# A list-scheduled opening for a T5 attention and bilinear feed-forward kernel, with pair 7 inside it and pads on two engines

## The chip, the cores and the metric

One core of a Trainium2 chip. The metric is device time in microseconds (us) of that core. The kernel before takes 417.34 us (median of 3 runs, 416.81 to 418.78).

## The reference

```python
# q, k, v: [8 batches, 8 heads, 576, 64]; bias_table: [32, 8]
scores = q @ k.T / 8 + bias_table[bucket(|i - j|)]       # T5 relative bias
attn   = softmax(scores) @ v
x      = attn.transpose(0, 2, 1, 3).reshape(4608, 512)   # [tokens, heads * 64]
out    = ((x @ w_a) * (x @ w_b)) @ w_out                 # d_ff = 1536
```

The kernel works on pairs of heads: pairs 0 to 3 are batch 0, 4 to 7 batch 1, up to 31. The softmax bias is a multiplication by exp(bias) after the exponential.

Of the kernel before, what the change touches and what calls it, by code (L numbers as in the profile page):

```python
# [13 lines left out]
def kernel(  # L14
# [11 lines left out]
    nc = tc.nc  # L26
# [7 lines left out]
    NM = 4  # L34
# [60 lines left out]
    vm = [wpool.tile([128, H, NM, Dh + 1], BF16, name=f"vm{i}") for i in range(2)]  # L95
    vt = [wpool.tile([128, H // 2, 2, Dh + 1], BF16, name=f"vt{i}") for i in range(2)]

# [70 lines left out]
    def load_vt(b):  # L168
        for hh in range(2):
            nc.gpsimd.dma_start(  # L170
                out=vt[b % 2][64 * hh:64 * hh + 64, :, hh, 0:Dh],
                in_=v[b, hh:H:2, SM:S, :].transpose([1, 0, 2]))
# [31 lines left out]

# [7 lines left out]
    nc.vector.memset(zero_sb[:, :], 0.0)  # L212
# [26 lines left out]

    nc.sync.dma_start(out=tab.ap(), in_=tab_sb[0:H, :])  # L240
    pad_vt(0)
    pad_ones(0)

# [5 lines left out]
    def load_vt_part(b, hh):  # L249
        nc.gpsimd.dma_start(  # L250
            out=vt[b % 2][64 * hh:64 * hh + 64, :, hh, 0:Dh],
            in_=v[b, hh:H:2, SM:S, :].transpose([1, 0, 2]))
# [85 lines left out]
    def copy_k(p, eng):  # L338
        copy(eng, KT[p % 4][:, :, :], st[p]["tk"][:, 0:SM].rearrange("d (t c) -> d t c", t=NM))

    def t_q(p, eng=None):
        if p >= NP or not early(p // 4):
            return
        ps = tr_half()
        transposes(ps, qn, p)
        copy(eng, QT[p % 4][:, :, :].rearrange("d a c -> d (a c)").rearrange("d (p t) -> d p t", t=NM),
             ps[:, 0:SM].rearrange("d (t p) -> d p t", t=NM))

    def t_k(p, eng=None, pool=None):
        if p >= NP or not early(p // 4):  # L350
            return
        ps = pool.tile([128, 1024], BF16, tag="ffn", name=f"trk{p}") if pool else tr_half()
        transposes(ps, kn, p)
        copy(eng, KT[p % 4][:, :, :], ps[:, 0:SM].rearrange("d (t c) -> d t c", t=NM))

# [198 lines left out]
    def av_mm(p, jqs, pool=None, tag="av"):  # L554
        b, hp = divmod(p, 4)
        i = b % 2
        pav = (pool or ps_av).tile([128, 3, 2, Dh + 1], FP32, tag=tag, name=f"av{p}_{jqs[0]}")
        for slot, jq in enumerate(jqs):
            nc.tensor.matmul(out=pav[:, slot, :, :], lhsT=weights_tail(p, jq),  # L559
                             rhs=vt[i][:, hp, :, :], start=True, stop=True)  # L560
            if jq == 4:
                for t in range(NM):
                    nc.tensor.matmul(out=pav[:, slot, :, :], lhsT=weights_last(p, t),  # L563
                                     rhs=vm[i][:, 2 * hp:2 * hp + 2, t, :], start=False,
                                     stop=True, skip_group_check=True)
# [25 lines left out]
    def t_x(p, jqs=range(5), eng=None):  # L591
        b, hp = divmod(p, 4)
        c0 = SM * B + ST * b
        if 4 <= p < NP - 1 and p != 7:
            nc.sync.dma_start_transpose(
# [77 lines left out]
    def ff_o_out(c, tt):  # L673
        ob = wrk.tile([128, DM], FP32, tag="ob", name=f"ob{c}_{tt}")
        nc.scalar.activation(out=ob[:, :], in_=ff["po", tt][:, :], func=ACTF.Copy)  # L675
# [15 lines left out]
    for c in range(NCH):  # L691
        if c == 0:
            parts = [(range(0, 8), 0, 256), (range(0, 8), 256, 256), (range(8, NDF), 0, 512)]
        else:
            parts = [(range(NDF), 0, 512)]
# [22 lines left out]
    def v_next(s):  # L718
# [9 lines left out]
    opening = """  # L728
        <k0 <q0 <q123h0 <tk <k23 <k1 <W0 <v0 <vtb <Wtb <W1 <W3 <vta <W2 <tq <R1 <q123h1 <v1 <R0 <Wta
        <wa0 <wb0 TK0 PD0 CK0:A PD1 w1 TQ0 PU1 CQ00:D CQ01:D w4 S000 w2 PU0 TQ20 E000 PC1 TQ10 S001 CQ20:D  # L730
        CQ10:D TQ30 E001 PC0 TZ1 CQ30:D S011 CZ1:A PC2 <vt1b <uq <vt1a <R2 <wa1 <q4 <R3 <k4 <wb1 <vb1b
        <q5 <k5 <uk <vb1a <wb2 <q6 <q7 <k6 <k7 <wa2 <wo S010 PF0 TK3 PF1 E011 TK2 CK3:D CK2:D E010 w1
        S300 M001 TK1 E300 M000 KS CK1:D EK w1 S101 V0:D E101 w1 S100 E100 M101 w1 S200 AV00 M300 E200 S301
        N00 TZ0 E301 M100 X00 S201 CX00:D AV10 wa4 E201 M200 N10 CZ0:A M201 X10 TQ11 M301 CX10:A T0 CQ11:A
        V1:D TQ31 ET0 S111 M010 AV20 E111 PW MT0 T1 N20 AV30 CQ31:A ET1 M011 TQ21 LH S110 N30 X20 CQ21:A
        S310 CX20:A MT1 X30 E110 AV01 CX30:D M111 FA0a E310 M110 S210 FB0a N01 HA0a S211 E210 FA1a G0a
        AV11 HA1a M210 E211 X01 T2 N11 TZ0x CX01:A T3 ET2 FB1a M211 X11 FA2a G1a CX11:A S311 MT2 HA2a
        FB2a ET3 CZ0x:D AV21 G2a E311 M310 TQ4 FA3a N21 CQ4:A TK4 FB3a HA3a CK4:D X21 FA4a G3a CX21:A
        S41 M311 HA4a S43 E41 MT3 FB4a FA5a E43 G4a AV31 LV M41 HA5a S40 V3:D S42 N31 E40 FB5a TQ5 G5a
        E42 X31 FA6a CQ5:D FB6a HA6a CX31:D TK5 G6a TZ1x CK5:A FA7a M40 FB7a HA7a CZ1x:D S52 S53 G7a E52  # L740
        FA0b V2:D FB0b M42 HA0b T4 E53 G0b FA1b M52 FB1b HA1b S50 M53 ET4 FA2b G1b TQ6 M43 HA2b S51
        CQ6:A FB2b MT4 E51 TQ7 G2b AV40 CQ7:D E50 TK6 M51 TK7 CK6:A FA3b M50 FB3b HA3b CK7:D S61 G3b T5
        E61 N40 FA4b FB4b HA4b M61 T6 ET5 G4b AV41 FA5b ET6 N41 TH S63 FB5b MT5 HA5b S62 E63 FA6b G5b MT6
        AV50 HA6b M63 E62 S60 FB6b N50 E60 FA7b G6b AV51 M62 HA7b FB7b M60 FA8f G7b N51 FB8f HA8f G8f
    """
# [4 lines left out]
    def step(token):  # L750
# [185 lines left out]
```

## The kernel before, where the change touches it

The first two batches are written out by hand as a list of tokens, executed in program order: each engine works through its own share of the list in that order. A tile scheduler puts in the waits. After the list comes a loop over the pairs `s`, which interleaves attention with nine feed-forward units for each pair.

```python
    vt = [wpool.tile([128, H // 2, 2, Dh + 1], BF16, name=f"vt{i}") for i in range(2)]
    ...
    def pad_vt(i):                                   # zeros beside V's tails, on DVE
        nc.vector.memset(vt[i][0:64, :, 1, :], 0.0)
        nc.vector.memset(vt[i][64:128, :, 0, :], 0.0)
    ...
    trb = ps_tr.tile([128, 1024], BF16, tag="tr", name="trb")   # one PSUM tile, used in halves
    def tr_half():
        turn[0] ^= 1
        return trb[:, 512 * turn[0]:512 * turn[0] + 512]
    ...
    def t_x(p, jqs=range(5), eng=None):
        ...
        if 4 <= p < NP - 1 and p != 7:               # pairs 4, 5, 6, 8 .. : by DMA transpose
            nc.sync.dma_start_transpose(out=xn_sb[hp][...], in_=XG[p % 2][...])
            ...
            return
        tr_x(p, jqs)                                 # the others: by PE and a copy
        copy_x(p, jqs, eng)
    ...
    opening = """
        <k0 <q0 <q123h0 <tk <k23 <k1 <W0 <v0 <vtb <Wtb <W1 <W3 <vta <W2 <tq <R1 <q123h1 <v1 <R0 <Wta
        <wa0 <wb0 TK0 PD0 CK0:A PD1 w1 TQ0 PU1 CQ00:D CQ01:D w4 S000 w2 PU0 TQ20 E000 PC1 TQ10 S001 CQ20:D
        CQ10:D TQ30 E001 PC0 TZ1 CQ30:D S011 CZ1:A PC2 ... S010 PF0 TK3 PF1 E011 TK2 CK3:D CK2:D E010 w1
        ... AV10 wa4 E201 M200 N10 ... FA0a E310 M110 S210 FB0a N01 HA0a ...
        ... AV51 M62 HA7b FB7b M60 FA8f G7b N51 FB8f HA8f G8f
    """
    ...
    for s in range(7, NP + 1):                       # pairs 7 .. 31, then the rest
        ...
```

How to read a token. `<x` starts a load. `TQ`, `TK`, `TZ`, `X` are transposes on PE (of queries, keys, tails, results), `CQ`, `CK`, `CZ`, `CX` their copies out of PSUM, with `:A` on ACT and `:D` on DVE. `S` are scores (PE), `E` their exponential (ACT), `M` the multiplication by the bias (DVE). `KS`, `EK` and `T`, `ET`, `MT` do the same for the 64 tail rows and columns. `AV` is the product with V, `N` its division by the sums (DVE). `FA`, `FB` are the feed-forward products pa and pb, `HA` (ACT) and `G` (DVE) join them; `w` are fill matmuls on zeros; `P…` write constant pads. `TH` starts batch 2's DMA transposes (among them QB, its queries), and the loop's first pair of batch 2 is pair 8.

The softmax here doesn't subtract the row's maximum and nothing guards it: scores larger than these inputs give would overflow.

## Time and profile before

| profile of the kernel before | us |
|---|---|
| first score (S000) | 6.97 |
| first pa / first pb of the feed-forward | 26.18 / 27.94 |
| first score of pair 8 | 73.69 |
| pair 8 to the end | 340.52 |
| span | 414.2 |

These milestones, from PE's timeline, cut the run into a start, a hand-written second half, and a loop both kernels share. The page's head says how full PE is (busy us, share, instructions):

```profile
span 414.2 us, 8826 instructions
...
PE 403.8 (97%) x3497; PEld 210.9 (51%) x3497; DVE 241.1 (58%) x568; ACT 251.3 (61%) x388; POOL 133.5 (32%) x191
```

PE has nearly no free time, so a change must cut PE's work, or the waits in the first 28 us. This is how ACT opens, in order of time (start, length, engine, line, operation; in brackets the idle time before and what ended it):

```profile
7.41 1.02 ACT L452 ACTIVATE ath<-qkh 128x1024 bf16<-128x1024 f32 x1 [1.40 <-PE qkh L446]
8.64 1.02 ACT L452 ACTIVATE ath<-qkh 128x1024 bf16<-128x1024 f32 x1 [0.21 <-PE qkh L446]
10.15 0.77 ACT L296 ACTIVATE ZB<-trb 64x256 bf16<-64x256 bf16 x2 [0.49 <-DVE QT L298]
10.94 2.86 ACT L452 ACTIVATE ath<-qkh 128x1024 bf16<-128x1024 f32 x3
```

The exponentials are `ath<-qkh`, 1.02 us each.

### The profile page before, as it was taken

The numbers are of one execution on the slowest core, as the hardware profiler recorded it, in microseconds if no ns is written. First come the engines' busy times: TensorE is split into PE (matmuls) and PEld (weight loads), VectorE is DVE, ScalarE is ACT, GpSimd is POOL, SyncE is SP. The second block draws the span as 40 slices with busy tenths as digits, with TensorE's granted clock in tenths as the row PEclk, the third lists the DMA queues.
The fourth block names the chain that finished last, engine by engine and source line by source line (L and its number), as shares of the span: only waits on it lengthen the run. The fifth ranks groups of instructions, "written<-read, shape, count | busy, mean of one in ns | idle before, by whom it ended". The sixth has DMA issues, their size and how long they took to land.

```text
span 414.2 us, 8826 instructions
## 1 busy us (share of the span) xinstructions
PE 403.8 (97%) x3497; PEld 210.9 (51%) x3497; DVE 241.1 (58%) x568; ACT 251.3 (61%) x388; POOL 133.5 (32%) x191
## 2 busy tenths in 40 slices
PE   8789999999999999999999999999999999999996
PEld 3467664545454455544555555554545555444443
DVE  5778887466764665477646774567646652421320
ACT  4988876486647676676667665866476742322321
POOL 7956546399209500870059003400000000000000
PEclk9999999999999999999999999999999999999999
DMA  9999999999949943996099707940421012002004
GB/s 116 171 210 191 205 157 144 164 142 138 123 96 163 121 82 71 150 128 112 15 162 157 112 16 140 124 92 17 101 82 16 17 40 78 0 2 102 1 2 101
DMA packets 135786, 42.05 MB, mean 102 GB/s; under 512 B 113688, under 2 KB 130968, under 8 KB 135744
## 3 DMA queue, kind: packets, MB, share of 16 engines
q0 software_dynamic: 81712, 20.27, 54.6%
q1 hardware_dynamic: 48592, 11.87, 18.1%
q10 hardware_dynamic: 5440, 9.34, 6.8%
q8 instruction: 27, 0.44, 0.5%
q14 instruction: 15, 0.12, 0.1%
HBM read 39.18 MB, written 9.45 MB: 117 GB/s over the span
## 4 chain that ended last, share of the span: by engine, by line
PE 90%; DMA 3%; POOL 2%; ACT 2%; issue 1%; ACTq 0%; DVE 0%
PE pb L633 23%; PE pa L633 23%; PE po L670 22%; PE av L569 7%; PE qk L406 7%; DMA wb<-in_moe_w_b_dram 3%; PE av L559 2%; PE av L563 2%; PE qkt L479 1%; POOL W L235 1%; DMA bias_tab<-wo 1%; PE trb L306 1%; PE trb L415 1%; PE warm L220 1%; ACT att L514 1%
## 5 line engine op out<-in xcount | busy, mean ns | idle before, releaser
L430 ACT ACTIVATE at<-qk 128x1024 bf16<-128x1024 f32 x112 | 113.5, 1030 | 26.4 <-PE qk L406 10.6
L643 DVE TENSOR_TENSOR g<-pb,ha 128x512 bf16<-128x512 f32 (+1 forms) x116 | 75.9, 654 | 74.7 <-PE pb L633 46.8
L633 PE MATMUL pb<-xn,wb 128*128 128x512 bf16 (+1 forms) x464 | 112.5, 365 | 0.8 <-DMA wb<-in_moe_w_b_dram 0.8
L633 PE MATMUL pa<-xn,wa 128*128 128x512 bf16 (+1 forms) x464 | 112.5, 365 | 0.0
L640 ACT ACTIVATE ha<-pa 128x512 f32<-128x512 f32 (+1 forms) x116 | 66.7, 575 | 65.0 <-PE pa L633 65.0
L670 PE MATMUL po<-wo,g 128*128 128x512 bf16 x420 | 99.0, 379 | 0.0
L435 DVE TENSOR_TENSOR at<-at,W 128x1024 bf16<-128x1024 bf16 x112 | 74.8, 684 | 18.2 <-ACT at L430 18.2
L633 PEld LDWEIGHTS <-wa 128*128 128x128 bf16 x464 | 42.0, 98 | 46.2 <-issue 6.0
L633 PEld LDWEIGHTS <-wb 128*128 128x128 bf16 x464 | 41.4, 97 | 43.0 <-issue 4.7
L670 PEld LDWEIGHTS <-g 128*128 128x128 bf16 x420 | 38.7, 98 | 44.0 <-issue 2.5
L675 ACT ACTIVATE ob<-po 128x512 f32<-128x512 f32 x35 | 21.1, 601 | 40.7 <-PE po L670 34.4
L569 PE MATMUL av<-vm,at 128*128 128x65 bf16 x896 | 41.2, 194 | 0.0
L170 POOL DMA_DIRECT2D vt<-in_v_dram x12 | 7.4, 621 | 104.1 <-PE av L563 103.2
L580 DVE RECIPROCAL rc<-av 128x6 f32<-128x6 f32 (+1 forms) x64 | 11.9, 186 | 49.5 <-PE av L569 43.8
L569 PEld LDWEIGHTS <-at 128*128 128x128 bf16 x896 | 37.2, 98 | 6.2
L132 POOL DMA_DIRECT2D qn<-in_q_dram x48 | 36.8, 832 | 9.9 <-PE pb L633 6.8
L141 POOL DMA_DIRECT2D kn<-in_k_dram x48 | 36.4, 820 | 2.0 <-PE pb L633 1.4
L559 PE MATMUL av<-vt,att 128*128 128x130 bf16 x152 | 33.3, 219 | 0.0
L406 PE MATMUL qk<-QB,KB 64*128 64x512 bf16 x192 | 29.2, 381 | 0.2 <-ACT att L506 0.2
L582 DVE TENSOR_TENSOR XG<-av,rc 128x384 bf16<-128x384 f32 (+1 forms) x64 | 27.1, 424 | 2.2
L506 ACT ACTIVATE att<-qkt 128x640 bf16<-128x640 f32 x24 | 16.9, 702 | 12.9 <-PE qkt L480 12.9
L559 PEld LDWEIGHTS <-att 128*128 128x128 bf16 x152 | 15.0, 98 | 6.4
(104 smaller groups left out, 325.2 us busy)
## 6 DMA issues: line engine op xcount, KB each, us to landing
out_dram<-ob ACTq DMA_DIRECT2D x32, 256.0 KB, 2.6
vn<-in_v_dram POOLq DMA_DIRECT2D x16, 256.0 KB, 5.6
kn<-in_k_dram POOLq DMA_DIRECT2D x48, 64.0 KB, 4.6
qn<-in_q_dram POOLq DMA_DIRECT2D x48, 64.0 KB, 4.3
wa<-in_moe_w_a_dram POOLq DMA_DIRECT2D x3, 512.0 KB, 9.3
wb<-in_moe_w_b_dram POOLq DMA_DIRECT2D x3, 512.0 KB, 10.4
wo<-in_moe_w_out_dram POOLq DMA_DIRECT2D x1, 1536.0 KB, 15.5
xn<-XG SPq DMA_TRANSPOSE x52, 4.1
```

Source lines behind the costliest of these rows:

```text
L132: nc.gpsimd.dma_start(out=by_tile(qn[b % 2])[:, h0 // 4, t, :, :], in_=q[b, h0:h1, 128 * t:128 * t + 128, :].transpose([1, 0, 2]))
L141: nc.gpsimd.dma_start(out=by_tile(kn[b % 2])[:, h0 // 4, t, :, :], in_=k[b, h0:h1, t:SM:NM, :].transpose([1, 0, 2]))
L406: nc.tensor.matmul(out=ps[:, hh, :], lhsT=kT[r, t, :], rhs=qT[r, :, :], start=True, stop=True)
L430: nc.scalar.activation(out=at[:, :, :], in_=ps[:, :, :], func=ACTF.Exp, scale=scale)
L435: nc.vector.tensor_tensor(out=at[:, :, :], in0=at[:, :, :], in1=w[:, :, S - 1 + t:S - 1 + t - SM:-1], op=MULT)
L559: nc.tensor.matmul(out=pav[:, slot, :, :], lhsT=weights_tail(p, jq), rhs=vt[i][:, hp, :, :], start=True, stop=True)
L569: nc.tensor.matmul(out=pav[:, slot, hh, :], lhsT=weights(p, t, hh, jq), rhs=vm[i][:, 2 * hp + hh, t, :], start=False, stop=True, skip_grou ...
L582: nc.vector.tensor_tensor(out=xg[:, jqs[0]:jqs[0] + m, :, :], in0=pav[:, 0:m, :, 0:Dh], in1=rc[:, 0:m, :].unsqueeze(3).to_broadcast([128, ...
L633: nc.tensor.matmul(out=ps[:, 0:n], lhsT=w[df // 4][:, mc, 128 * (df % 4):128 * (df % 4) + 128], rhs=xn_sb[mc][:, 512 * c + lo:512 * c + lo ...
L640: nc.scalar.activation(out=ha[:, 0:n], in_=ff["pa", df, lo][:, 0:n], func=ACTF.Copy)
L643: nc.vector.tensor_tensor(out=g_sb[df][:, lo:lo + n], in0=ff["pb", df, lo][:, 0:n], in1=ff["ha", df, lo][:, 0:n], op=MULT)
L670: nc.tensor.matmul(out=po[:, :], lhsT=g_sb[df][:, 128 * tt:128 * tt + 128], rhs=wo_sb[:, df, :], start=(df == 0), stop=(df == NDF - 1))
```

## The change

It replaces the hand order of the opening by that of a list scheduler: exponentials close together at the start, 22 fills cut to 13, fewer changes of tile form, pair 7 wholly inside the opening, another load order, and pads that either copy engine can write. The diff, cut to its core (helpers, dead code and most tokens left out):

```diff
-    vt = [wpool.tile([128, H // 2, 2, Dh + 1], BF16, name=f"vt{i}") for i in range(2)]
+    vt = [wpool.tile([128, 2, H // 2, Dh + 1], BF16, name=f"vt{i}") for i in range(2)]
 ...
+    def pad(eng, x, p0, p1):
+        if eng is nc.vector:
+            nc.vector.memset(x, 0.0)
+            return
+        ...
+        nc.scalar.activation(out=x, in_=z, func=ACTF.Copy)      # z: a view of the zeros
 ...
-        if 4 <= p < NP - 1 and p != 7:
+        if 4 <= p < NP - 1:
 ...
-            parts = [(range(0, 8), 0, 256), (range(0, 8), 256, 256), (range(8, NDF), 0, 512)]
+            parts = [(range(0, 6), 0, 256), (range(0, 6), 256, 256), (range(6, NDF), 0, 512)]
 ...
     opening = """
-        <k0 <q0 <q123h0 <tk <k23 <k1 <W0 <v0 <vtb <Wtb <W1 <W3 <vta <W2 <tq <R1 <q123h1 <v1 <R0 <Wta
-        <wa0 <wb0 TK0 PD0 CK0:A PD1 w1 TQ0 PU1 CQ00:D CQ01:D w4 S000 w2 PU0 TQ20 E000 PC1 TQ10 S001 CQ20:D
+        <k0 <q0 <tk <q123h0 <k23 <k1 <tq <vta <R0 <W1 <vtb <W0 <q123h1 <v0 <W3 <W2 <v1 <Wta <Wtb <k4 <R1
+        <uq <wa0 <wb0 ... PV0:A PF1:D PF0:D TK0 PV1:D TQ0 CQ00:D PU1:A w1 TZ1 CK0:A CQ01:A PX1:D S000 E000 PC1:D
+        CZ1:D S001 E001 TQ30 S011 TQ10 TK3 PX0:D CK3:D TK2 E011 CQ10:D CK2:D PU0:D S010 CQ30:A S301 TK1
 ...
+        S210 E210 S211 E211 M110 TQ31 LH N01 MT1 X01 T2 ET2 N30 AV11 CQ31:D X30
+        CX30:A T3 ET3 CX01:D S311 FA0a HA0a N11 E311 TZ0x FB0a ...
 ...
+        E73 M73 AV51 N51 TH T7 M72 ... AV70 ... N70 AV60 ... X70 ... AV71 CX70:D ... CX71:A ... FO02 HO0
 ...
-    for s in range(7, NP + 1):
+    for s in range(8, NP + 1):
```

More of the change, by code (lines that the diff above doesn't have):

```diff
@@ L170, in load_vt @@
             nc.gpsimd.dma_start(
-                out=vt[b % 2][64 * hh:64 * hh + 64, :, hh, 0:Dh],
+                out=vt[b % 2][64 * hh:64 * hh + 64, hh, :, 0:Dh],
                 in_=v[b, hh:H:2, SM:S, :].transpose([1, 0, 2]))
@@ L191, in pad_tl, with pad_vt, pad_blocks, pad_x @@
         nc.vector.memset(tl[i][64:128, :, :, 0:Dh], 0.0)
-    def pad_vt(i):
-        nc.vector.memset(vt[i][0:64, :, 1, :], 0.0)
-        nc.vector.memset(vt[i][64:128, :, 0, :], 0.0)
+    def pad(eng, x, p0, p1):
+        if eng is nc.vector:
+            nc.vector.memset(x, 0.0)
+            return
+        n = int(np.prod(x.shape[1:]))
+        z = (zero_sb.bitcast(FP32) if x.dtype == FP32 else zero_sb)[p0:p1, 0:n]
+        if len(x.shape) == 3:
+            z = z.rearrange("p (a b) -> p a b", b=x.shape[2])
+        elif len(x.shape) == 4:
+            z = z.rearrange("p (a b c) -> p a b c", b=x.shape[2], c=x.shape[3])
+        nc.scalar.activation(out=x, in_=z, func=ACTF.Copy)
+    def pad_vt(i, hh, eng):
+        pad(eng, vt[i][64 * hh:64 * hh + 64, 1 - hh, :, :], 64 * hh, 64 * hh + 64)
+    def pad_blocks(x, hh, eng):
+        o = (Dh - Dh * hh) // 2
+        pad(eng, x.bitcast(FP32)[64 * hh:64 * hh + 64, :, :, o:o + Dh // 2], 64 * hh, 64 * hh + 64)
     def pad_ones(i):
-        nc.vector.memset(vt[i][0:64, :, 0, Dh:Dh + 1], 1.0)
-        nc.vector.memset(vt[i][64:128, :, 1, Dh:Dh + 1], 1.0)
+        nc.vector.memset(vt[i][0:64, 0, :, Dh:Dh + 1], 1.0)
+        nc.vector.memset(vt[i][64:128, 1, :, Dh:Dh + 1], 1.0)
         nc.vector.memset(vm[i][:, :, :, Dh:Dh + 1], 1.0)
-    def pad_x(i):
-        nc.vector.memset(XG[i][64:128, 4, :, :], 0.0)
+    def pad_x(i, eng):
+        pad(eng, XG[i][64:128, 4, :, :], 64, 128)
     nc.sync.dma_start(out=bt_sb[0:NB, :], in_=bias_table)
@@ L213 @@
     nc.vector.memset(tab_sb.bitcast(FP32)[0:H, :], TWO_ONES)
+    pad_ones(0)
+    pad_ones(1)
     nc.vector.tensor_tensor(out=bt_sb[0:NB, :], in0=bt_sb[0:NB, :], in1=bl_sb[0:NB, :],
@@ L240 @@
     nc.sync.dma_start(out=tab.ap(), in_=tab_sb[0:H, :])
-    pad_vt(0)
-    pad_ones(0)
     def load_wt(hh):
@@ L250, in load_vt_part @@
         nc.gpsimd.dma_start(
-            out=vt[b % 2][64 * hh:64 * hh + 64, :, hh, 0:Dh],
+            out=vt[b % 2][64 * hh:64 * hh + 64, hh, :, 0:Dh],
             in_=v[b, hh:H:2, SM:S, :].transpose([1, 0, 2]))
@@ L339, in copy_k @@
         copy(eng, KT[p % 4][:, :, :], st[p]["tk"][:, 0:SM].rearrange("d (t c) -> d t c", t=NM))
-    def t_q(p, eng=None):
-        if p >= NP or not early(p // 4):
-            return
-        ps = tr_half()
-        transposes(ps, qn, p)
-        copy(eng, QT[p % 4][:, :, :].rearrange("d a c -> d (a c)").rearrange("d (p t) -> d p t", t=NM),
-             ps[:, 0:SM].rearrange("d (t p) -> d p t", t=NM))
-    def t_k(p, eng=None, pool=None):
-        if p >= NP or not early(p // 4):
-            return
-        ps = pool.tile([128, 1024], BF16, tag="ffn", name=f"trk{p}") if pool else tr_half()
-        transposes(ps, kn, p)
-        copy(eng, KT[p % 4][:, :, :], ps[:, 0:SM].rearrange("d (t c) -> d t c", t=NM))
     tz = {}
@@ L559, in av_mm @@
             nc.tensor.matmul(out=pav[:, slot, :, :], lhsT=weights_tail(p, jq),
-                             rhs=vt[i][:, hp, :, :], start=True, stop=True)
+                             rhs=vt[i][:, :, hp, :], start=True, stop=True)
             if jq == 4:
@@ L673, in ff_o_out @@
     def ff_o_out(c, tt):
-        ob = wrk.tile([128, DM], FP32, tag="ob", name=f"ob{c}_{tt}")
+        ob = ob_last if (c, tt) == (0, 2) else wrk.tile([128, DM], FP32, tag="ob", name=f"ob{c}_{tt}")
         nc.scalar.activation(out=ob[:, :], in_=ff["po", tt][:, :], func=ACTF.Copy)
@@ L728 @@
     opening = """
-        <k0 <q0 <q123h0 <tk <k23 <k1 <W0 <v0 <vtb <Wtb <W1 <W3 <vta <W2 <tq <R1 <q123h1 <v1 <R0 <Wta
-        <wa0 <wb0 TK0 PD0 CK0:A PD1 w1 TQ0 PU1 CQ00:D CQ01:D w4 S000 w2 PU0 TQ20 E000 PC1 TQ10 S001 CQ20:D
-        CQ10:D TQ30 E001 PC0 TZ1 CQ30:D S011 CZ1:A PC2 <vt1b <uq <vt1a <R2 <wa1 <q4 <R3 <k4 <wb1 <vb1b
-        <q5 <k5 <uk <vb1a <wb2 <q6 <q7 <k6 <k7 <wa2 <wo S010 PF0 TK3 PF1 E011 TK2 CK3:D CK2:D E010 w1
-        S300 M001 TK1 E300 M000 KS CK1:D EK w1 S101 V0:D E101 w1 S100 E100 M101 w1 S200 AV00 M300 E200 S301
@@ L734 @@
-        N00 TZ0 E301 M100 X00 S201 CX00:D AV10 wa4 E201 M200 N10 CZ0:A M201 X10 TQ11 M301 CX10:A T0 CQ11:A
-        V1:D TQ31 ET0 S111 M010 AV20 E111 PW MT0 T1 N20 AV30 CQ31:A ET1 M011 TQ21 LH S110 N30 X20 CQ21:A
-        S310 CX20:A MT1 X30 E110 AV01 CX30:D M111 FA0a E310 M110 S210 FB0a N01 HA0a S211 E210 FA1a G0a
-        AV11 HA1a M210 E211 X01 T2 N11 TZ0x CX01:A T3 ET2 FB1a M211 X11 FA2a G1a CX11:A S311 MT2 HA2a
-        FB2a ET3 CZ0x:D AV21 G2a E311 M310 TQ4 FA3a N21 CQ4:A TK4 FB3a HA3a CK4:D X21 FA4a G3a CX21:A
@@ L739 @@
-        S41 M311 HA4a S43 E41 MT3 FB4a FA5a E43 G4a AV31 LV M41 HA5a S40 V3:D S42 N31 E40 FB5a TQ5 G5a
-        E42 X31 FA6a CQ5:D FB6a HA6a CX31:D TK5 G6a TZ1x CK5:A FA7a M40 FB7a HA7a CZ1x:D S52 S53 G7a E52
-        FA0b V2:D FB0b M42 HA0b T4 E53 G0b FA1b M52 FB1b HA1b S50 M53 ET4 FA2b G1b TQ6 M43 HA2b S51
-        CQ6:A FB2b MT4 E51 TQ7 G2b AV40 CQ7:D E50 TK6 M51 TK7 CK6:A FA3b M50 FB3b HA3b CK7:D S61 G3b T5
-        E61 N40 FA4b FB4b HA4b M61 T6 ET5 G4b AV41 FA5b ET6 N41 TH S63 FB5b MT5 HA5b S62 E63 FA6b G5b MT6
@@ L744 @@
-        AV50 HA6b M63 E62 S60 FB6b N50 E60 FA7b G6b AV51 M62 HA7b FB7b M60 FA8f G7b N51 FB8f HA8f G8f
+        <k0 <q0 <tk <q123h0 <k23 <k1 <tq <vta <R0 <W1 <vtb <W0 <q123h1 <v0 <W3 <W2 <v1 <Wta <Wtb <k4 <R1
+        <uq <wa0 <wb0 <q4 <R3 <q7 <R2 <k5 <q5 <k6 <wa1 <vt1b <uk <wb1 <k7 <vt1a <q6 <vb1a <wa2 <wb2
+        <vb1b <wo PV0:A PF1:D PF0:D TK0 PV1:D TQ0 CQ00:D PU1:A w1 TZ1 CK0:A CQ01:A PX1:D S000 E000 PC1:D
+        CZ1:D S001 E001 TQ30 S011 TQ10 TK3 PX0:D CK3:D TK2 E011 CQ10:D CK2:D PU0:D S010 CQ30:A S301 TK1
@@ new lines @@
+        E010 E301 CK1:D TQ20 CQ20:D M011 M010 w1 S100 E100 M100 TZ0 CZ0:D S101 E101 M101 w2 S300 E300 w2
+        S200 KS TQ11 M001 TQ21 M000 E200 V0:D CQ11:D S201 EK M300 T0 M301 E201 ET0 AV00 N00 CQ21:A M201
+        S110 AV10 S111 N10 X00 X10 E110 M200 T1 V1:A AV20 CX00:A PW:D MT0 CX10:A TK4 N20 E111 AV30 CK4:A
+        AV01 ET1 M111 X20 CX20:A S210 E210 S211 E211 M110 TQ31 LH N01 MT1 X01 T2 ET2 N30 AV11 CQ31:D X30
+        CX30:A T3 ET3 CX01:D S311 FA0a HA0a N11 E311 TZ0x FB0a FA1a CZ0x:D G0a X11 TQ4 HA1a S310 CX11:A
@@ new lines @@
+        MT3 CQ4:D M311 FB1a G1a E310 M310 FA2a M211 HA2a TQ7 CQ7:A S43 M210 E43 S41 E41 FB2a G2a FA3a
+        TK5 TQ5 AV31 CQ5:D FB3a S42 N31 CK5:A S51 HA3a MT2 M43 FA4a X31 TK6 E42 HA4a E51 G3a CK6:D AV21
+        LV CX31:A S52 E52 N21 S53 E53 PC0:D FB4a G4a FA5a TK7 X21 HA5a FB5a M42 S50 E50 CX21:D S40 FA0b
+        G5a FB0b HA0b CK7:D M41 TQ6 E40 G0b TZ1x CZ1x:D FA1b HA1b S71 CQ6:D FB1b E71 G1b V2:D FA2b HA2b
+        T4 ET4 M40 FB2b G2b S70 MT4 FA3b FB3b M51 T6 HA3b AV40 E70 FA4b HA4b M71 T5 G3b N40 M53 FB4b G4b
@@ L745 @@
+        FA5b ET5 MT5 HA5b AV41 ET6 FB5b G5b FA6f FB6f N41 HA6f S61 E61 S72 FA7f E72 HA7f M52 M50 AV50
+        G6f M70 M61 V3:A FB7f N50 S73 S62 FA8f MT6 G7f E73 M73 AV51 N51 TH T7 M72 FB8f HA8f G8f E62 M62
+        S63 ET7 MT7 FA9f S60 E63 FB9f HA9f M63 E60 AV70 G9f M60 FA10f FB10f HA10f N70 AV60 G10f N60 X70
+        FA11f HA11f AV71 CX70:D FB11f FO00 N71 AV61 X71 CX71:A G11f N61 FO01 FO02 HO0
     """
@@ L819, in step @@
             av_norm(p, jqs)
-            if not first and i[1] == 1:
+            if 4 <= p < 7 and i[1] == 1:
                 t_x(p)
@@ L825, in step @@
             copy_x(p, jqs, eng)
+        elif kind == "PV":
+            pad_vt(0, p, eng)
+        elif kind == "PC":
+            pad_vt(1, p, eng)
         elif kind == "PU":
-            pad_z(1, p)
+            pad_blocks(ZB[1], p, eng)
         elif kind == "PF":
-            nc.vector.memset(tl[0][64 * p:64 * p + 64, :, :, Dh - Dh * p:128 - Dh * p], 0.0)
-        elif kind == "PC":
-            if p == 2:
-                pad_ones(1)
-            else:
-                nc.vector.memset(vt[1][64 * p:64 * p + 64, :, 1 - p, :], 0.0)
+            pad_blocks(tl[0], p, eng)
+        elif kind == "PX":
+            pad_x(p, eng)
         elif kind == "PW":
-            nc.vector.tensor_copy(out=Wt_sb[:, :, 0:64], in_=Wt_sb[:, :, 64:128])
-        elif kind == "PD":
-            pad_x(p)
+            copy(eng, Wt_sb[:, :, 0:64], Wt_sb[:, :, 64:128])
         elif kind == "LH":
@@ L851 @@
     pad_tl(1)
-    quotas = {7: 9, 8: 9}
     load_slot = {bb: 9 if bb == 3 else 12 if bb == 4 else 4 * bb - 5 for bb in range(3, B)}
-    for s in range(7, NP + 1):
+    for s in range(8, NP + 1):
         new = s < NP
         U = "unit"
-        A = lambda *jq: (lambda: av(s - 1, jq))
+        A = lambda *jq: (lambda: av(s - 1, jq) if s > 8 else None)
         steps = []
@@ L862 @@
         if new:
-            head = [U, lambda: ex(s, 1), A(0, 1, 2), U, lambda: mul(s, 0), lambda: t_q(s + 1), U,
+            head = [U, lambda: ex(s, 1), A(0, 1, 2), U, lambda: mul(s, 0), U,
                     lambda: mul(s, 1)]
@@ L866 @@
             if s == 8:
-                late = [A(3, 4), U, lambda: t_x(7, (0, 1, 2)), U, lambda: t_x(7, (3, 4))]
-            if shared(s):
-                pair = [lambda: v_next(s), lambda: (qk(s, 2), ex(s, 2), ex_rows(s)), U,
-                        lambda: ex(s, 3), U, lambda: mul(s, 2), lambda: mul_rows(s)]
-            else:
-                pair = [lambda: v_next(s), lambda: (qk(s, 2), ex(s, 2)), U, lambda: ex(s, 3),
-                        lambda: t_k(s + 1, ACT), U, lambda: mul(s, 2)]
+                late = [U]
+            pair = [lambda: v_next(s), lambda: (qk(s, 2), ex(s, 2), ex_rows(s)), U,
+                    lambda: ex(s, 3), U, lambda: mul(s, 2), lambda: mul_rows(s)]
             tail = [lambda: (qk_tail(s), ex_tail(s)), U, U, lambda: mul_tail(s)]
@@ L893 @@
                     load_half(bb, g)
-        quota = quotas.get(s, 9)
+        quota = 9
         seen, put = 0, 0
```

## The prediction

> **What bounds the kernel now.** I read the page's chain of work first, then stretches of each engine, then the tensor engine in order of time, then the load queue. The chain is matmuls almost throughout:
>
> ```profile
> PE 90%; DMA 3%; POOL 2%; ACT 2%; issue 1%; ACTq 0%; DVE 0%
> ```
>
> The stretches (columns: length, then busy us of PE, PEld, DVE, ACT, POOL; clock; DMA share; GB/s) tell where it is not:
>
> ```profile
> 7.00:16.00 9.00, 6.78 (x95) 3.68 (x94) 5.51 (x18) 7.86 (x10) 8.93 (x13) 1.00 1.19 170
> 16.00:26.00 10.00, 8.80 (x166) 6.51 (x165) 9.19 (x25) 8.99 (x16) 7.17 (x11) 1.00 1.21 183
> 28.00:40.00 12.00, 11.81 (x166) 8.72 (x166) 9.72 (x27) 9.11 (x19) 8.95 (x13) 1.00 1.35 198
> 64.00:74.00 10.00, 10.00 (x88) 5.11 (x86) 6.76 (x16) 5.92 (x10) 4.88 (x7) 1.00 1.70 153
> ```
>
> From 7 to 26 us no engine is full alone: ACT has 7.86 of 9, then DVE 9.19 of 10, and PE's busy time contains fill matmuls on zeros. From 28 us PE is full. So only the first 28 us hold much to win. Three places of PE's timeline cut the run (start, length, engine, line):
>
> ```profile
> 1.19 2.31 PE L220 MATMUL warm<-zero_sb 128*128 128x512 bf16 x5 [1.19 <-DVE zero_sb L212]
> ...
> 26.18 0.60 PE L633 MATMUL pa<-xn,wa 128*128 128x256 bf16 x4
> 26.71 0.39 PE L446 MATMUL qkh<-QT,KT 64*128 64x256 bf16 x4
> 27.94 0.61 PE L633 MATMUL pb<-xn,wb 128*128 128x256 bf16 x4 [0.83 <-DMA wb<-in_moe_w_b_dram]
> ...
> 73.69 0.61 PE L406 MATMUL qk<-QB,KB 64*128 64x512 bf16 x4
> ```
>
> They are PE's first matmul; the first pb of the feed-forward, which waits for wb; and the first score of pair 8, from which both programs run the same loop. Busy time hides gaps, since ends are modelled. So I took the spacing with which each kind of matmul follows itself in the trace (512 columns 216 ns, 256: 109, 130: 57, 128: 55.5, 65: 32, 64: 29; two half-array matmuls side by side count once) and added 96 ns for each change of tile form (a 256-column matmul before a 64-row one takes 205 ns instead of 109). By this count PE's own work is 19.08 us up to the first pb and 43.69 us from there to pair 8. The trace took 26.75 and 45.75. So 7.67 us of waiting lie before the first pb and 2.06 us after it; after pair 8 I count 1.3 us in 326 us.
>
> [...] The first five fills follow one another at 427 ns, the same fill from 6 us at 216[...]. [...] the trace's 64x256 ACT copies took 0.38. [...] the stretches show 170 to 214 GB/s from 5 to 55 us, and wb, issued at 17.43 us, landed only at 27.89.
>
> **The change, part by part.** From the compiled order of both programs:
> - Fills. 22 fill matmuls before pair 8 become 13: 9 x 0.216 = 1.94 us less PE work.
> - Grouping. Changes of tile form before pair 8 fall from 81 to 68: 13 x 0.096 = 1.25 us less.
> - Pair 7's products with V and its transposes move ahead of pair 8: 1.82 us of PE work that leave the loop. Nothing is saved by the move itself.
> - The split of chunk 0 (6 instead of 8 blocks by halves) keeps the columns.
> So PE's work to the first pb is 19.10 (as good as 19.08, fewer fills but more attention), from there to pair 8 42.26 (43.69 before), and over the program 3.2 us less. If waits stayed as they are the gain would be 3.2 us.
>
> - Pads. One 64x260 and one 64x256 memset (0.28 and 0.27 us on DVE) go to ACT, before its first exp, while ACT is idle (1.40 and 2.22 us idle in the trace): free. The ones move into DVE's wait of 0.91 us for the bias row, also free.
> - Scores. ACT's first three exps start at 7.41, 8.64 and 10.94 us now; fills, a transpose and the key-tail copies stand between. Afterwards S000, S001, S011 are adjacent and the tail copies are DVE's: I expect about 7.3, 8.2, 9.1. ACT's twelfth item of this sort then comes about 1.1 us earlier. But batch 0's third-pair keys (k23, landing 9.69) hold TK3 and what stands behind it.
> - Loads. W0 was 7th in the queue, v0 8th; now they are 12th and 14th. I map landing time to bytes queued ahead, from the trace: 896 KB 10.37 us, 1282 KB 12.90, 1540 KB 15.07, 1832 KB 16.01, 2248 KB 18.58, 2760 KB 21.46, 3272 KB 24.36, 3784 KB 27.89, 4072 KB 29.06. The new order puts W0 at 1444 KB, about 14.0 us (was 10.73), v0 at 1892 KB, 16.3 us (was 12.90), and, as k4 and the batch 1 query tails (192 KB) now stand before the first weights, wb at 3976 KB, 28.7 us (was 27.89).
> - DVE's chain. Its first bias multiplications need W0: they ran at 11.83 us, now not before 14.0. It then has, in order up to N30 (the last quarter of batch 0's first half): 12 multiplications at 0.605 = 7.3, the norms 3.2, two tail multiplications 1.4, copies, tails and values 2.5, together 14.2 to 14.5 us, so N30 ends near 28.3, its transpose and ACT copy near 28.9. The first pa starts near 29 (26.18 before), the first pb near 29.3 (27.94 before): 1.36 us later, although ACT is ahead.
>
> After that DVE has about 39 us of work in PE's 44 (it is at 10.77 of 12 in its fullest stretch now); the loads for pairs 5 to 7 and the later weights land, by the same map, at or just before their use (wa1 36.3, wb1 39.6, k7 40.3 us against needs at about 36.4, 39.7 and 40.5). I leave the waits there at 2.0 us.
>
> The sum: first pb +1.36; work to pair 8 42.26 - 43.69 = -1.43; waits there -0.06; pair 7's work off the loop -1.82. Together -1.95 us: 417.34 - 1.95 = 415.4 us.
>
> **Rivals.** (a) The start is bound by ACT and the rearranged exps carry through: DVE's 14 us were read too pessimistically or W0 lands near 12.5, and pb waits for wb only. Then pb starts near 28.0 to 28.7 and, with 1 us of waits after it, the span falls by 3.5 to 4.2 us: about 413.3. For it: ACT is at 7.86 of 9 and 8.99 of 10. Against it: DVE at 9.19 of 10 with the loads earlier than they will be. (b) New waits in the second half: pair 7 inside the opening must write XG while pair 5's DMA transposes (5 to 8 us from issue to landing in the trace) still read it, and batch 2's transposes are issued after pair 5's, some 10 us before pair 8; each could cost 1 to 2 us, for about 418. For it: the transpose of the queries took 7.7 us from issue. Against it: the author put two feed-forward blocks before N70. (c) Fewer fills let the clock fall back while DVE waits for W0[...], 417 to 418. For it: PE's work between the first score and the first product with V is 7.0 us in a stretch of about 12. [...]
>
> **Range and chances.** The gain cannot pass 2% (8.3 us): all waiting before pair 8 is 9.7 us, and wb's landing near 28 keeps about 8 us of it unless the load queue itself gets faster. A loss of 2% would need three rivals at once. Predicted 415.4 us; 412.6 to 417.9 should hold it 8 times in 10. Chances: faster by over 2% 0.03, within 2% 0.95, slower 0.02.
>
> **What would show it.** In the changed profile: fills down by nine; first exps at 7.3, 8.2, 9.1; DVE idle before its first bias multiplication near 14 us, named as waiting for W; first pa near 29 and first pb near 29.3, DVE full between; PE from there to pair 8 in about 44.3 us; the loop from pair 8 1.8 us shorter. If pb starts before 28 us, or pair 8 later than 75 us, the steps on DVE and loads, or on the later waits, were wrong.

The rate of the loads is 162 to 214 GB/s in the trace's stretches of 5 us from 5 to 55 us.

## The result, and the profile after

Ratios here are the mean time of one kernel's runs over that of the other's of the same rounds, so they are not quite the ratio of the quoted medians. Executions over 1.5% slower than the fastest of the same kernel are left out of the means.

| | median of runs, us | before, same rounds | ratio (95%) |
|---|---|---|---|
| first measurement | 415.28 (414.56 to 415.87) | 417.07 (416.21 to 418.78) | 0.9952 (0.9929 to 0.9976) |
| the same kernel again, another job | 415.9 (415.07 to 417.21) | 416.61 (416.29 to 417.6) | 0.9988 (0.9973 to 1.0002) |

The gain is small, between 0.1 and 0.5%. It is within 2%, as predicted; the first median lies 0.1 us from the predicted time, but the repeat 0.5 us, and the repeat's interval just touches one. The profiled execution after was its job's slowest of six (415.87 us), so its span hardly differs from that of before:

```profile
span 414.1 us, 8776 instructions
...
PE 405.5 (98%) x3472; PEld 210.0 (51%) x3472; DVE 240.8 (58%) x565; ACT 252.7 (61%) x387; POOL 133.5 (32%) x191
...
PE 90%; DMA 3%; ACT 2%; DVE 1%; issue 1%; POOL 1%; SPq 1%; ACTq 0%; POOLq 0%
```

25 matmuls fewer, yet PE is busy 1.7 us longer: busy time is no work count, since part of it ran at half clock (two fills took 1.04 us there, 0.60 at full clock; below). The stretches of after (length, busy us of PE, PEld, DVE, ACT, POOL; clock; DMA share; GB/s):

```profile
7.00:16.00 9.00, 8.16 (x86) 3.87 (x82) 4.90 (x13) 7.33 (x9) 8.32 (x13) 1.00 1.26 175
16.00:26.00 10.00, 8.79 (x158) 6.23 (x157) 8.83 (x22) 9.47 (x14) 7.93 (x12) 1.00 1.29 203
28.00:40.00 12.00, 11.97 (x174) 8.53 (x173) 10.49 (x30) 10.86 (x19) 7.47 (x12) 1.00 1.40 200
64.00:74.00 10.00, 9.70 (x117) 6.03 (x116) 7.00 (x21) 2.79 (x6) 5.05 (x8) 1.00 1.72 144
```

The clock of 1.00 in the first row is only a default: this trace's first clock record, of full clock, starts at 17.2 us. From 16 to 26 us ACT is now the fullest engine (9.47 of 10; DVE 8.83), where I had put DVE. From 64 to 74 us PE is no longer full (9.70; it was 10.00). PE's milestones of after, in its timeline:

```profile
30.12 0.61 PE L633 MATMUL pa<-xn,wa 128*128 128x256 bf16 x4
30.88 0.61 PE L633 MATMUL pb<-xn,wb 128*128 128x256 bf16 x4
...
67.78 0.23 PE L559 MATMUL av<-vt,att 128*128 128x130 bf16 x1 [0.30 <-DVE XG L582]
...
75.22 0.61 PE L406 MATMUL qk<-QB,KB 64*128 64x512 bf16 x4 [0.48 <-DMA QB<-qn]
```

The first pb comes at 30.88 us with no wait for wb any more; pair 8's first score waits for batch 2's DMA transpose QB, and a product with V waits for DVE to write XG. The page's chain of work (the waits that end last, followed back) names that transpose as a long piece (start, length):

```profile
65.58 9.60 DMA QB<-qn
```

Put side by side, with a second profile of each kernel from the next job:

| us | before | before again | after | after again |
|---|---|---|---|---|
| first pb | 27.94 | 28.20 | 30.88 | 30.28 |
| first pb to pair 8 | 45.75 | 45.75 | 44.34 | 44.16 |
| pair 8 to the end | 340.52 | 340.52 | 338.84 | 338.86 |
| span | 414.2 | 414.5 | 414.1 | 413.3 |

The second half and the loop give 1.50 and 1.67 us, repeatably. The start takes 2.51 us of it back (means 30.58 against 28.07). The rest, -0.66 us, is the mean difference of the spans.

Why the start is late shows in ACT's timeline of after. First its early part, then the end of it:

```profile
7.36 2.89 ACT L452 ACTIVATE ath<-qkh 128x1024 bf16<-128x1024 f32 x3
10.99 0.38 ACT L311 ACTIVATE QT<-trb 128x256 bf16<-128x256 bf16 x1 [0.74 <-DVE QT L313]
11.27 1.94 ACT L452 ACTIVATE ath<-qkh 128x1024 bf16<-128x1024 f32 x2
14.07 1.94 ACT L452 ACTIVATE ath<-qkh 128x1024 bf16<-128x1024 f32 x2 [0.87 <-PE qkh L446]
16.22 1.02 ACT L452 ACTIVATE ath<-qkh 128x1024 bf16<-128x1024 f32 x1 [0.21 <-PE qkh L446]
17.54 1.02 ACT L452 ACTIVATE ath<-qkh 128x1024 bf16<-128x1024 f32 x1 [0.29 <-PE qkh L446]
...
19.36 1.03 ACT L452 ACTIVATE ath<-qkh 128x1024 bf16<-128x1024 f32 x1
```

```profile
28.63 0.93 ACT L514 ACTIVATE att<-qkt 128x896 bf16<-128x896 f32 x1
29.51 0.38 ACT L311 ACTIVATE xn<-trb 128x256 bf16<-128x256 bf16 x1
```

Three exponentials run in one piece from 7.36 us, as intended. Then ACT loses 0.74, 0.87, 0.21 and 0.29 us, 2.11 together, so that its eleventh exponential-sized item (E201, the prediction's "twelfth") starts at 19.36 us, against 18.22 before. The last two of these gaps stand behind scores and fills that PE ran at half clock (four scores in 0.61 us, two fills in 1.04 and 1.03; shown below, with the fills). From 17.54 us on ACT has no gap to speak of, and the copy of the last quarter of the first half chunk (`xn<-trb`, token CX30) stands behind a tail exponential: it ends at 29.89, and pa starts at 30.12.

With both profiles of each kernel, the 2.51 us come from three stretches:

| mean of two profiles, us | before | after | difference |
|---|---|---|---|
| start to the first exponential | 7.78 | 7.11 | -0.67 |
| first exponential to E201 | 10.81 | 11.94 | +1.13 |
| E201 to the first pb | 9.48 | 11.53 | +2.05 |

So most of the delay arises after E201, where ACT's list is longer. Ahead of CX30 it now has the value copy V1 (1.06 us), the key copy CK4 (0.61), the exponentials E210 and E211 (1.94) and one tail exponential (0.93), which before stood later or on DVE: 4.5 us more, against a tail copy (0.76), two query copies and about 1 us of idle time that are gone. From E201 to the start of CX30 it takes 10.15 us in place of 6.51. In seven profiles of the changed order that leave this part of the list as it is, the experiments' included, E201 to pb takes 11.52 to 11.56 us, whenever E201 comes.

The 0.74 us is a wait between two engines that read one tile: ACT's copy CQ30 reads one half of `trb`, DVE's CQ10 the other half, and ACT waits for DVE. What puts the two in this order is not shown. DVE is late because its queue has a key copy ahead. Its timeline of after:

```profile
10.14 0.42 DVE L313 COPY KT<-trk 128x512 bf16<-128x512 bf16 x1 [2.13 <-PE trk L321]
...
12.67 0.42 DVE L313 COPY KT<-trk 128x512 bf16<-128x512 bf16 x1 [1.18 <-PE trk L321]
...
13.40 1.29 DVE L461 TENSOR_TENSOR ath<-ath,W 128x1024 bf16<-128x1024 bf16 x2
```

DVE waits 2.13 and 1.18 us for PE's key transposes; its first bias multiplications, at 13.40 us, wait for nothing. W0 had landed at 12.90 us, 0.50 us earlier (0.25 us in the second profile): it did not hold them here, but not by much.

### The profile page after: what moved, and what is told of

The parts are those of the page before. It is cut to its first block, busy times and chain, and to the rows that moved or that the text cites. A ratio compares the mean times of both kernels' runs of the same rounds, so it can differ in the third digit from the quotient of the medians.

```text
span 414.1 us, 8776 instructions
## 1 busy us (share of the span) xinstructions
PE 405.5 (98%) x3472; PEld 210.0 (51%) x3472; DVE 240.8 (58%) x565; ACT 252.7 (61%) x387; POOL 133.5 (32%) x191
## 4 chain that ended last, share of the span: by engine, by line
PE 90%; DMA 3%; ACT 2%; DVE 1%; issue 1%; POOL 1%; SPq 1%; ACTq 0%; POOLq 0%
PE pa L633 22%; PE pb L633 22%; PE po L670 22%; PE av L569 7%; PE qk L406 7%; DMA QB<-qn 2%; PE av L559 2%; PE av L563 2%; PE qkt L479 1%; DMA qn<-in_q_dram 1%; ACT ath L452 1%; PE qkh L446 1%; PE trb L321 1%; PE warm L237 1%; PE trb L415 1%
## 5 line engine op out<-in xcount | busy, mean ns | idle before, releaser
L582 DVE TENSOR_TENSOR XG<-av,rc 128x384 bf16<-128x384 f32 (+2 forms) x64 | 27.2, 425 | 3.0 <-DMA xn<-XG 0.9
## 6 DMA issues: line engine op xcount, KB each, us to landing
wo<-in_moe_w_out_dram POOLq DMA_DIRECT2D x1, 1536.0 KB, 15.5
```

The lines of the kernel that those rows point to most:

```text
L582: nc.vector.tensor_tensor(out=xg[:, jqs[0]:jqs[0] + m, :, :], in0=pav[:, 0:m, :, 0:Dh], in1=rc[:, 0:m, :].unsqueeze(3).to_broadcast([128, ...
```

## The experiments

Theory on reading the result: the start is held by ACT's queue (the wait for DVE's copy, waits for scores, and CX30 behind a tail exponential), the fills were never a cost, and the QB and XG waits eat into the second half. Rivals: DVE waiting for W0, as predicted; a clock that falls to half with fewer fills; simply noise between jobs. In the tables "ratio" is against the kernel before in the same job.

### First job: noise and fills (before: 416.61 us, 11 runs, 416.29 to 417.6)

**The changed kernel again**, unedited.

> The changed kernel unchanged, for a second profile. In its first profile (a run of 415.87 us, the slowest of six) the early matmuls have the spacing of the half clock until about 17 us: two fills at 14.60 and at 16.11 us take 0.97 us each pair instead of 0.53. Theory C (the clock's warming is a matter of luck after the change, since few fills stand after 5 us): another profile can show the fills at 216 ns from about 5 us on and then the first pb before 30.0 us; time 414.5 to 415.9 us. Rival (the change itself always leaves the clock cold): cold until 16 us again and pb at 30.9 us.

Measured 415.9 us, ratio 0.9988 (0.9973 to 1.0002). PE's timeline of this run:

```profile
74.44 0.61 PE L406 MATMUL qk<-QB,KB 64*128 64x512 bf16 x4 [0.16 <-DMA QB<-qn]
```

The clock was not at half until 16 us this time, nor at full throughout: by the trace's clock records the array has full clock from 5.3 to 8.8 us, half clock to 15.6, then full (a mean of 0.62 from 7 to 16 us), where the first profile records full clock only from 17.2 us. So the theory of luck is half right, and the first pb, at 30.28, missed its mark of 30.0. The first exponential came 0.5 us earlier (6.87 against 7.36), but from ACT's copy CQ30 (11.00 and 10.99 us) to its exponentials at 14.09 and 14.07 the two profiles agree; the 0.6 us at E201 (18.75 against 19.36) and at pb arise in the stretch where only the first is still at half clock (two fills at 16.11 us take 1.03 us there, at 15.91 us 0.61 here).

The milestones stand within 0.8 us, but the timed gain is 0.7 us in place of 1.8. The two intervals only just overlap: the ratio of one and the same kernel differs by 0.36% between two jobs, as much as the whole gain.

**Seven fills put back into the changed kernel**, all in places where PE waits.

```diff
-PU1:A w1 TZ1        -S001 E001 TQ30      -TQ10 TK3      -S010 CQ30:A S301      -S201 EK
+PU1:A w2 TZ1        +S001 E001 w2 TQ30   +TQ10 w2 TK3   +S010 w1 CQ30:A S301   +S201 w1 EK
```

> The changed kernel with 7 fills put back into places where its tensor engine waited (after the first query copy, after S001, TQ10, S010 and S201). Theory C: the array is warm by 9 us at the latest in every run, the cold stretch to 17 us goes, first pb 0.5 to 1.5 us earlier than in e1, time 0.3 to 1.2 us below e1. Rival 1 (the prediction's step: each fill is 0.216 us of work on the path): 7 x 0.216 = 1.5 us slower than e1. Rival 2: the start is held by ACT and DVE, fills lie in waits: within 0.3 us of e1.

Measured 416.0 us (413.52 to 417.18), ratio 0.9975 (0.9952 to 0.9998): the same as without them. Its first pb is at 30.39 us, pair 8 at 75.58. The clock did change. First PE's timeline of the changed kernel, then of this one:

```profile
14.60 1.04 PE L237 MATMUL warm<-zero_sb 128*128 128x512 bf16 x2
15.57 0.61 PE L446 MATMUL qkh<-QT,KT 64*128 64x256 bf16 x4
16.11 1.03 PE L237 MATMUL warm<-zero_sb 128*128 128x512 bf16 x2
17.08 0.41 PE L446 MATMUL qkh<-QT,KT 64*128 64x256 bf16 x4
```

```profile
15.70 0.60 PE L237 MATMUL warm<-zero_sb 128*128 128x512 bf16 x2
16.29 0.40 PE L446 MATMUL qkh<-QT,KT 64*128 64x256 bf16 x4
```

Two fills take 1.04 us and four score matmuls 0.61 in the changed kernel until 17.1 us, 0.60 and 0.40 with more fills: its array was at half clock, this one's, at full clock from 9.3 us on, not. So the third rival of the prediction is real. The first pb came no earlier than in the repeat (30.39 against 30.28 us), but that does not show that the half clock costs nothing, as ACT's timeline of this run tells:

```profile
8.30 2.89 ACT L452 ACTIVATE ath<-qkh 128x1024 bf16<-128x1024 f32 x3
...
12.42 5.65 ACT L452 ACTIVATE ath<-qkh 128x1024 bf16<-128x1024 f32 x6
```

Six exponentials run in one piece, and from the first exponential to E201 it took 10.53 us in place of 12.00 and 11.88. That was used up because the first exponential came at 8.30 instead of 7.36 and 6.87: the queries landed 0.55 us later, and two fills at half clock (1.03 us, at 6.47) stood before it. How much of the shorter stretch is the clock, and how much only ACT's later start, this one profile can't say.

**Nine fills taken out of the kernel before.**

```diff
-CQ01:D w4 S000 w2 PU0      -AV10 wa4 E201
+CQ01:D w1 S000 PU0         +AV10 E201
```

> The kernel before with 9 fills taken out (3 ahead of S000, 2 after it, 4 after AV10), so that it has the changed kernel's number, 13. If the fills were work on the path: 1.9 us faster than before. If they lay in waits: within 0.3 us. If they hold the clock: a cold stretch after 6 us in its profile and up to 1 us slower.

Measured 416.8 us (416.68 to 417.56), ratio 1.0006 (0.9994 to 1.0018). 1.94 us of PE work gone, no time gained. Both directions agree: the fills lie in waits. The cold stretch that the expectation names, one at half clock, came too: in its profile (a run of 417.56 us, the slowest of five) the array is at half clock from 8.7 to 12.1 and from 19.0 to 25.8 us (four scores take 0.61 us at 11.57 and at 22.49, in place of 0.39 to 0.40), and the first pb is at 29.46 us, against 27.94 and 28.20 with the fills. The kernel before, with these fills, has full clock in its trace's records from 5.4 us on. So there, too, the clock fell with fewer fills; the times don't show a cost.

**The kernel before again**, as a candidate, to learn what the comparison gives for nothing.

> The kernel before unchanged: what two times of the same kernel differ by, and a second profile of it. Ratio 1.000 within 0.002; fills at 216 ns from 5 to 6 us on if its clock does not depend on luck, first pb near 27.9 us.

Measured 416.42 us, ratio 0.9996 (0.9984 to 1.0008). Its first pb still waits for wb:

```profile
28.20 0.61 PE L633 MATMUL pb<-xn,wb 128*128 128x256 bf16 x4 [0.34 <-DMA wb<-in_moe_w_b_dram]
```

### Second job: the waits one by one (before: 416.49 us, 416.21 to 417.23)

**Pair 5's results transposed by PE instead of DMA**, so that XG and the transpose queue come free sooner.

```diff
-        if 4 <= p < 7 and i[1] == 1:      -N50         -AV51 N51 TH
+        if p in (4, 6) and i[1] == 1:     +N50 X50 CX50:A   +AV51 N51 X51 CX51:A TH
```

> The changed kernel, with pair 5's output transposed on the tensor engine (as pair 7's already is) instead of by two DMA transposes. In all three profiles of the changed order PE waits 0.3 to 1.7 us in the product of pair 6 (XG, not yet read by pair 5's DMA transposes) and 0.16 to 0.48 us for QB at pair 8, because batch 2's transposes stand behind pair 5's. Theory T (the end of the opening is held by the DMA transposes): both waits go, pair 8 begins 0.5 to 1.5 us earlier, time 0.3 to 1.2 us below the changed kernel. Rival D (the late first pb alone makes the gain small): only the 0.28 us of added PE work, no gain.

Measured 416.7 us, ratio 0.9999 (0.9988 to 1.0011): no gain left. QB now lands at 67.15 us, 9 us ahead of its use, but pair 8 begins at 76.33 us, later and not earlier: PE's timeline shows other waits in its place (one of 0.27 us at 58.73, and this one):

```profile
61.79 0.59 PE L609 MATMUL trb<-ident,XG 128*128 128x128 bf16 x2 [0.60 <-DVE XG L582]
```

PE's transposes stand directly behind the norms that feed them, and PE works in the order of the list. That was my placement, not the idea; the third job moves them.

**The copy CX30 ahead of the tail exponentials.**

```diff
-S211 E211 M110 TQ31 LH N01 MT1 X01 T2 ET2 N30 AV11 CQ31:D X30 CX30:A T3 ET3 CX01:D S311 FA0a HA0a N11
+S211 M110 N30 X30 CX30:A E211 TQ31 LH N01 MT1 X01 FA0a HA0a T2 ET2 AV11 CQ31:D T3 ET3 CX01:D S311 N11
```

> The changed kernel, with the last norm of the first half (N30), its transpose and its copy moved ahead of N01, MT1 and the tail exponentials that stood in front of it on DVE and ACT, and the first pa behind it. Theory D (first pb late by ACT and DVE order): first pa about 1.5 us earlier (28.3 instead of 29.5 to 30.1). If the end is then held by the DMA transposes (theory T), the time stays within 0.4 us of the changed kernel, although pa is earlier; if not, about 1 us faster.

Measured 415.48 us (414.76 to 416.32), ratio 0.9970 (0.9958 to 0.9983): between the changed kernel's two ratios. PE's timeline:

```profile
28.23 0.60 PE L633 MATMUL pa<-xn,wa 128*128 128x256 bf16 x4
...
30.90 0.61 PE L633 MATMUL pb<-xn,wb 128*128 128x256 bf16 x4
...
75.89 0.61 PE L406 MATMUL qk<-QB,KB 64*128 64x512 bf16 x4 [1.27 <-DMA QB<-qn]
```

The first pa does come 1.3 to 1.9 us earlier, so CX30 behind the exponentials was what held it (E201 to pa took 9.23 us, in place of 10.76). But the tail work then stands before pb, which does not move, and the wait for QB has grown to 1.27 us.

**Both query copies on DVE, ahead of the key copies**, so that ACT never waits for the shared tile.

```diff
-TQ30 S011 TQ10 TK3 PX0:D CK3:D TK2 E011 CQ10:D CK2:D PU0:D S010 CQ30:A S301
+TQ30 CQ30:D S011 TQ10 CQ10:D S010 TK3 PX0:D CK3:D TK2 E011 CK2:D PU0:D S301
```

> The changed kernel, with the query copies of pairs 3 and 1 done by DVE as soon as they are transposed (DVE idles 2.1 to 2.5 us there) and S010 ahead of TK3. ACT's wait of 0.7 to 0.95 us in front of its fourth exp goes; the items up to E201 come about 1 us earlier. Theory D: first pa 0.5 to 1 us earlier; time 0 to 1 us faster.

Measured 414.53 us (413.12 to 415.69), ratio 0.9946 (0.9931 to 0.9962). ACT's timeline shows four exponentials in one piece and no wait for DVE's copy:

```profile
7.42 3.77 ACT L452 ACTIVATE ath<-qkh 128x1024 bf16<-128x1024 f32 x4
```

Its profile fell on the slowest of its six runs, and there the first pb is at 31.74 us and the span 413.9. In it W0 landed only at 15.54 us, and DVE did wait for it:

```profile
15.67 1.90 DVE L461 TENSOR_TENSOR ath<-ath,W 128x1024 bf16<-128x1024 bf16 x3 [2.77 <-DMA W<-bias_tab]
```

From E201 to pb it then took 12.81 us in place of 11.5, which fits the predicted step holding pb here. The timed advantage over the kernel before is shown; by which step it arises is not.

**All three edits together.**

> The three edits together. If T and D both hold: first pa near 27.5 us, pair 8 near 72.5 us instead of 74.4 to 75.6, time 1.5 to 2.5 us below the changed kernel, near 413 us. If the loads (wb lands at 26.7 to 27.9 us) or PE's own work bind: less than 1 us.

Measured 417.27 us (416.27 to 417.32), ratio 1.0008 (0.9996 to 1.0019): the gains do not add. It contains the first, bad placement of pair 5's transposes, so that it says little against the other two edits. The first pa came early (27.61 us), pb as late as ever (30.28), and pair 8 at 75.99.

### Third job: W0, pads, and a better place for pair 5 (before: 416.55 us, 415.86 to 417.27)

**W0 and v0 early in the load queue**, the test of the predicted cause.

```diff
-<tq <vta <R0 <W1 <vtb <W0 <q123h1 <v0 <W3
+<tq <vta <W0 <R0 <v0 <W1 <vtb <q123h1 <W3
```

> The changed kernel, with W0 and v0 loaded earlier (W0 ahead of R0, v0 ahead of W1), near their places in the kernel before. By the prediction's step (W0, expected at 14.0 us, holds DVE's first bias multiplication and with it the first pb): first pb about 1 us earlier, about 1 us faster. Theory D (in the profile that multiplication, at 13.4 us, waits for nothing; ACT is full from 17.5 to 30 us and sets the first pb): first pb and time unchanged within 0.4 us.

Measured 416.01 us (414.93 to 416.95), ratio 0.9979 (0.9961 to 0.9998). DVE's first bias multiplication did not come earlier, and still waits for no load:

```profile
14.42 1.29 DVE L461 TENSOR_TENSOR ath<-ath,W 128x1024 bf16<-128x1024 bf16 x2
```

W0 landed 0.8 us earlier (12.10), but the first pb of this profile is at 32.09 us. Another load explains the first part of that, the keys k23, which landed at 10.42 us instead of 9.38; PE's timeline:

```profile
10.47 1.06 PE L321 MATMUL trk<-ident,kn 128*64 128x128 bf16 x16 [1.02 <-DMA kn<-in_k_dram]
```

The array was then at half clock until 19.2 us (two fills take 1.04 us at 17.12). So W0 is not what holds the start of the changed kernel in its own two profiles. It is nearly tied, though: besides the 2.77 us above, DVE waited for it 0.41 to 0.63 us in the profiles of three other variants.

**The two ACT pads back on DVE.**

```diff
-PV0:A      -PU1:A
+PV0:D      +PU1:D
```

> The changed kernel, with the two pads that it gave to ACT back on DVE (0.28 and 0.27 us). DVE has idle time before and after the first query copy (0.4 and 0.7 us) in the profile, so I expect the first score to begin at most 0.3 us later and the time to stay within 0.4 us. If the padding's spread matters: 0.5 us or more slower.

Five runs of 414.32 to 416.8 us, ratio 0.9970 (0.9951 to 0.9989), again between the two ratios of the changed kernel: where these pads stand makes no difference that can be seen. The sixth run, the profiled one, took 818.01 us and can't be compared; its span is 816.2 us. One group of its lines view (busy us, mean ns):

```profile
L633 PE MATMUL pb<-xn,wb 128*128 128x512 bf16 x408 | 208.9, 672 | 0.0
```

The same matmul has a mean of 379 ns in the changed kernel's profile. So this run's matmuls were slow throughout. Why stays open: its trace has no record of the granted clock at all, so the 1.000 that its cores view prints is only a default.

**Pair 5 on PE, placed later.**

```diff
-E73 M73 AV51 N51 TH                  -G8f E62 M62
+E73 M73 X50 CX50:A AV51 N51 TH       +G8f E62 X51 CX51:A M62
```

> As f1, but with the two transposes of pair 5 standing later in the tensor engine's order, where their norms are long done. In f1 QB landed at 67.2 us instead of 74.4 to 75.2, yet PE lost about 2 us in waits in front of the two transposes. Theory T: without those waits pair 8 begins near 74.0 us, and the time is 0.3 to 1 us below the changed kernel. If copies on ACT and DVE simply cost what the DMA did: no gain, 415.5 to 416.5 us.

Measured 415.14 us (414.58 to 415.95), ratio 0.9965 (0.9951 to 0.9978). QB landed at 67.46 us and neither wait is left; PE's timeline:

```profile
74.69 0.61 PE L406 MATMUL qk<-QB,KB 64*128 64x512 bf16 x4
```

From the first pb (30.76) to pair 8 it took 43.93 us, with pair 5's transposes inside, against 44.16 and 44.34.

**This with the query copies on DVE.**

> f3 and f5 together. f3 alone was 0.54% faster than the kernel before (414.5 us). If its edit and the freed DMA queue add up: 413.5 us; if f3's advantage was noise between jobs (0.3%) it stays at 415 to 416 us.

Measured 414.29 us (414.0 to 415.62), ratio 0.9948 (0.9933 to 0.9962); first pb 30.36, pair 8 at 74.30, span 412.4. With the copies-on-DVE version of the second job this is the best. Both are clearly faster than the kernel before. That they beat the changed kernel is likely (414.3 and 414.5 against 415.3 and 415.9 us), but they were not timed beside it.

## Why the prediction was right, and where it was not

- **The time.** 415.4 predicted; 415.28 and 415.9 measured, both well inside the range. That the sum landed within 0.1 us is luck, by a favourable first job: the profiles' parts give -0.66 us, the timed differences -1.79 and -0.71, and the predicted sum was -1.95.
- **First pb, +1.36.** The sign was right and the size was not: +2.51 us. This is the term that was mis-sized, by 1.15 us. The step behind it failed: "its first bias multiplications need W0 … now not before 14.0". They started at 13.40 with no wait, W0 landed at 12.90 instead of 14.0, and loading W0 earlier brought nothing; only where it landed at 15.5 does it seem to have held pb. What ran in its place is ACT's list: 2.05 of the 2.51 us arise from E201 to pb, where 4.5 us of work moved ahead of CX30 on ACT. I had also taken ACT to be "ahead" by 1.1 us at E201; it was 1.1 us behind in the first pair of profiles (19.36 against 18.22) and level in the second (18.75 against 18.97), through waits of 2.11 us that I had not looked for, one of them between two engines reading one tile (0.74), two behind an array at half clock (0.21 and 0.29). Moving CX30 shows that ACT's order held the first pa; that more than pa must move before pb does, the same run shows. No run moves V1, CK4 or the two exponentials alone, so their shares are read from the traces and not tested.
- **wb at 28.7.** It landed at 27.1 and 26.7 us in the two profiles, so the map from bytes to landing time was 1.6 to 2.0 us late there. No wait for wb remains because everything else is later.
- **First exponentials at 7.3, 8.2, 9.1.** Measured 7.36, 8.28, 9.22, and in the repeat 6.87, 7.77, 9.10: right.
- **Fills, 1.94 us, and forms, 1.25 us.** The work is gone, but "3.2 us if waits stayed as they are" was the wrong condition. The fills stood in waits by design, so their removal turns into more waiting: both fill experiments show no time for 1.5 to 1.9 us of fills. Only what is saved in the full stretch counts.
- **First pb to pair 8, 44.3 us.** Measured 44.34 and 44.16: right. The waits by name, QB and XG, come to 0.78 and 0.60 us of the 2.0 left there; the rest has no name.
- **Pair 7 off the loop, 1.82 us.** Measured 1.67: right in kind and nearly in size.
- **Pads free.** Right as far as the timing can tell. The two pads took 0.40 and 0.41 us on ACT, in idle time.
- **Rivals.** (a), ACT as the bound, was half right: ACT is the bound, but it became slower, not faster. (b), QB and XG, is real and small: 0.16 to 0.48 us for QB in two profiles of the changed kernel and 0.30 to 0.44 for XG (up to 1.27 and 1.70 in the variants, QB with CX30 moved, XG with more fills). (c), the clock's fall with fewer fills, happened (half clock until 17.2 us, and from 8.8 to 15.6 in the repeat); in the start it goes with 0.6 us between the two profiles of the changed kernel, and no timing shows its cost.
- **Still open.** Why the loop from pair 8 is another 0.7 us shorter (338.1 against 338.85) in the three versions with pair 5 on PE alone or with the query copies (338.5 with CX30 moved, pair 5 on PE or not), what the half clock costs in time, and where the copies-on-DVE version gains, since its only profile is of its slowest run.

## What to carry to other kernels

Count saved work only where the engine never waits; here fill matmuls taken out of waits only made the waits longer (nine of them, 1.94 us, gave a ratio of 1.0006), and the clock fell (half clock from 8.7 to 12.1 and from 19.0 to 25.8 us in that run). When work moves to another engine, look at what it now stands ahead of there. A list schedule for several engines should also know the queue of DMA transposes (QB took 9.60 us from issue to landing) and the waits between two engines that read one tile (0.74 us here), or it moves the path onto one of these. Loads in one and the same order land about 1 us apart here (W0 12.90 to 13.97 us in most profiles, once 15.54), so a path with less slack than that can change from run to run. For a gain of a few tenths of a per cent, measure the same kernel in a second job before believing it: here the two jobs said 0.48 and 0.12%.
